# The sums of a windowed softmax: taken from ScalarE's accumulator instead of VectorE's reduction

## The chip, the cores and the metric

The kernel runs on one core of a Trainium2 chip. The metric is the time of one execution on the device, in microseconds (us); the span is the time from the first to the last instruction of the profiled execution. The engines are TensorE (PE; its weight loads are shown apart as PEld), VectorE (DVE), ScalarE (ACT), GpSimd (POOL) and SyncE (SP, which issues the transfers). Each engine works through its own queue in order and waits on semaphores for the others.

## The reference

Attention with a window and block summaries, and then two feed-forward layers on its result. Of the attention (2 batches, 8 heads, 768 positions, head size 64):

```python
scores_l = scale * np.matmul(q, k.transpose(0, 1, 3, 2))
mask_l = np.abs(pos[:, None] - pos[None, :]) < window            # window = 16
scores_s = scale * np.einsum('bhsd,bhnd->bhsn', q, k_sum) + np.log(block)
scores_all = np.concatenate([np.where(mask_l, scores_l, -1e9), scores_s], axis=-1)
scores_all = scores_all - np.max(scores_all, axis=-1, keepdims=True)
a = np.exp(scores_all)
a = a / (np.sum(a, axis=-1, keepdims=True) + 1e-09)
attn = np.matmul(a, np.concatenate([v, v_sum], axis=2))
```

Its 1536 x 512 result goes through `relu(x @ w_in) ** 2 @ w_out` (inner size 2048), and that through a second layer with a rational function in place of the squared relu.

## The kernel before

**The attention** is cut into 24 steps `d`, each for 2 x 128 queries of two heads. A step works on four slices `c` of 64 queries of two heads (128 rows) by 120 columns: 96 keys around the window and 24 block summaries. Its parts, with the letter that each has in the order below, are:

- `q`, `z`: PE transposes the queries, ACT copies them into `qz` (L445).
- `s`: PE makes the scores (four slices into one bank `pss`, L456).
- `m` (`d_m`, L471): per slice, DVE adds the mask, negates, and takes the minimum into column `c` of a small tile `mx` (128 x 8); the result goes to `pr`, a tile of 4 x 121 columns of which the last of each slice holds 1e-9.
- `e` (`d_e`, L480): per slice, ACT takes the exponential of `pr` in place, with column `c` of `mx` as bias. Below, e0 to e23 are these 24 groups of four exponentials.
- `r` (`d_r`, L488 and L489): DVE sums the 4 x 121 columns of `pr` into columns 4 to 7 of `mx` and takes the reciprocal into `rs`.
- `n` (L495): POOL multiplies the slices by `rs`; `p` (L505): PE transposes them; `b` (L509): ACT or DVE copies them to `pp`; `o` (L521): PE multiplies with the values; `x`, `y` (L535, L540): ACT casts the result to `xh`, DVE makes the remainder `xl`.

There are two buffers of `mx` and `rs` and three of `pr`.

**The feed-forward layers** multiply in three passes (high by high, high by low, low by high). `h` (L572) is the first multiplication of a layer, `i` (L585, ACT) its relu, `j` (L602, DVE) the square, `G` (L635, ACT) the cast to `sh`, `H` (L642, POOL) the remainder `sl`, `Y` (L666) the second multiplication. The weights arrive as 64-bit numbers and are made into a high and a low part by `T` (ACT, L150), `D` (DVE, L160 and L161), `W` (ACT, L172) and `M` (POOL, L177).

**The order** of attention, weights and the first layer's first pass is written out by hand in one string, `ORDER`, of a letter and a number for each part; each engine's queue follows it. After the string's end (at about 155 us) loops issue the rest. Near the start the string reads `... z5 s4 w0 p1 m4 o0 e4 r3 I1 I2 s5 z6 n2 Q2 p2 b1* B3* N2 T1 o1 m5 W0 ...`: W0 stands behind e0 to e4 in ACT's queue.

Of the kernel before, what the change touches and what calls it, by code (L numbers as in the profile page):

```python
# [12 lines left out]
ALU = mybir.AluOpType  # L13
I32 = mybir.dt.int32
AX = mybir.AxisListType
# [43 lines left out]
def tile_window_attention_moe_moe(  # L59
# [13 lines left out]
    nc = tc.nc  # L73
# [313 lines left out]
    def k_put(p, wins=slice(0, NWIN), copy=nc.vector.tensor_copy, first=True):  # L387

        p %= NP
        ks = kss[p]  # L390
        if first:
            nc.vector.tensor_reduce(
                out=ks.rearrange("p (w n) -> p w n", n=2),
                in_=kt[p][:, :, WIN:WIN + LO].rearrange("p w (n t) -> p w n t", t=BLK),
                axis=AX.X, op=ALU.max,
            )
        dst = kt[p][:, wins, WT:]
        copy(
            out=dst, in_=ks.rearrange("p (o n) -> p o n", o=1).to_broadcast([P, dst.shape[1], NB])
        )  # L400
# [76 lines left out]
    def d_e(d):  # L477
        mx, pr = ex[d] = pm.pop(d)
        for c in range(4):
            nc.scalar.activation(  # L480
                out=pr[:, c, 0:HK], in_=pr[:, c, 0:HK], func=AF.Exp, scale=-1.0,
                bias=mx[:, c:c + 1],
            )

    def d_r(d):
        mx, pr = ex.pop(d)
        rs = ap.tile([P, 4], F32, tag="rs", name="rs", bufs=2)
        nc.vector.tensor_reduce(out=mx[:, 4:8], in_=pr, axis=AX.X, op=ALU.add)  # L488
        nc.vector.reciprocal(out=rs, in_=mx[:, 4:8])  # L489
        pn[d] = rs, pr  # L490

# [229 lines left out]
    def w_next(j):  # L721
# [10 lines left out]
        c=lambda p: k_put(p, some, dve), B=lambda p, c=act: k_put(p, rest, c, False),  # L732
        S=lambda p: s_add(v0[p], LEFT) if p < NP else s_add(vst), V=v_sum,
        u=lambda h, c=act: v_put(h, 0, c), w=lambda h, c=act: v_put(h, 1, c),
        q=d_t, z=d_z, s=d_s, m=d_m, e=d_e, r=d_r, n=d_n, p=d_p, b=d_b, o=d_o, x=d_x, y=d_y,
        T=lambda k: w_next(0), D=lambda k: w_next(1), W=lambda k: w_next(2),
        M=lambda k: w_low(*divmod(k, 2)), O=lambda i: keep(("y0", "y1")),
# [47 lines left out]
    for g in range(G1, NG):  # L785
        ps, c, f = steps[g]
# [66 lines left out]
```

## Time and profile before

| | us |
|---|---|
| median of 3 runs | 620.4 (620.27 to 620.71) |
| profiled execution | 620.43 |
| its span | 618.5 |
| PE busy in the span | 600.2 (97%) |
| DVE busy / ACT busy / POOL busy | 407.6 / 403.2 / 356.4 |

The shares are averages over stages with different limits: the attention occupies the first 155 us, and the engines' shares there differ from those of the rest. PE's matmuls are pipelined, so a busy PE can still contain short waits.

### The profile page before, as it was taken

Reading aid. Unit: us, or ns where it says so; the run is one execution under the profiler, and the core shown is the slowest. Engines: PE = TensorE matmul, PEld = TensorE weight load, DVE = VectorE, ACT = ScalarE, POOL = GpSimd, SP = SyncE. Lnnn points to the kernel's source line nnn. Section 1 sums busy time; section 2 is a strip of 40 time slices with the busy share of each in tenths; the row PEclk is TensorE's granted clock in tenths of the full one; section 3 lists DMA queues with packets and bytes.
Section 4 is the critical chain, followed back from the end, with each engine's and each line's share of the span. In section 5 each row is a group of like instructions: output and inputs, shape, how many; then the busy total and the mean of one; then the engine's idle time right before and its main releaser. Section 6 shows DMA issues by size and latency. Waiting matters only on the chain.

```text
span 618.5 us, 9770 instructions
## 1 busy us (share of the span) xinstructions
PE 600.2 (97%) x3488; PEld 515.6 (83%) x3488; DVE 407.6 (66%) x810; ACT 403.2 (65%) x771; POOL 356.4 (58%) x363
## 2 busy tenths in 40 slices
PE   6789999999999999999999999999999999999997
PEld 5689999999988778888888888788888888888886
DVE  5988967855267762011247899978766977776673
ACT  5978667856265553112356998988778788777761
POOL 3878974545266665121477899855545754544451
PEclk9989999999999999999999999999999999999999
DMA  9979991730045550000016442310000000010011
GB/s 222 244 206 222 232 224 17 188 87 3 1 143 163 173 190 13 0 1 0 1 37 205 135 135 86 121 33 1 1 0 1 34 1 1 1 40 29 1 68 68
DMA packets 64143, 51.48 MB, mean 83 GB/s; under 512 B 39776, under 2 KB 56160, under 8 KB 64096
## 3 DMA queue, kind: packets, MB, share of 16 engines
q1 hardware_dynamic: 64096, 50.87, 30.5%
q8 instruction: 27, 0.44, 0.3%
q14 instruction: 20, 0.16, 0.1%
HBM read 47.71 MB, written 3.15 MB: 82 GB/s over the span
## 4 chain that ended last, share of the span: by engine, by line
PE 50%; DVE 7%; POOL 3%; ACT 2%; issue 1%; POOLq 0%; ACTq 0%; DVEq 0%
PE y L666 25%; PE h L572 25%; DVE wdec L161 2%; POOL wl L177 2%; POOL sl L642 1%; DVE acc L694 1%; DVE h L621 1%; ACT wdec L150 1%; DVE wdec L160 1%; DVE q L618 1%; DVE p L624 1%; DVE p L606 1%; DVE p L605 1%; ACT sh L635 0%; ACT wh L172 0%
## 5 line engine op out<-in xcount | busy, mean ns | idle before, releaser
L572 PE MATMUL h<-xh,wh 128*128 128x512 f32 (+1 forms) x444 | 162.3, 365 | 0.8 <-DVE r L602 0.4
L572 PE MATMUL h<-xl,wh 128*128 128x512 f32 (+1 forms) x444 | 160.1, 361 | 0.8 <-DVE xl L540 0.8
L572 PE MATMUL h<-xh,wl 128*128 128x512 f32 (+1 forms) x444 | 160.0, 360 | 0.0
L642 POOL TENSOR_TENSOR sl<-r,sh 128x512 fp32r<-128x512 f32 (+1 forms) x63 | 69.1, 1098 | 113.0 <-ACT sh L635 95.5
L593 POOL TENSOR_TENSOR q<-q,u 128x512 f32<-128x512 f32 x48 | 63.6, 1326 | 76.2 <-ACT q L590 76.2
L177 POOL TENSOR_TENSOR wl<-wdec,wh 128x512 fp32r<-128x512 f32 x64 | 87.5, 1375 | 25.6 <-ACT wh L172 25.6
L572 PEld LDWEIGHTS h<-xh,wh 128*128 128x128 f32 x444 | 83.7, 189 | 14.7 <-DVE p L624 1.1
L572 PEld LDWEIGHTS h<-xl,wh 128*128 128x128 f32 x444 | 83.8, 189 | 13.5 <-DVE xl L540 1.0
L602 DVE TENSOR_TENSOR r<-r,h 128x512 f32<-128x512 f32 (+1 forms) x63 | 35.0, 556 | 90.3 <-ACT r L585 90.3
L572 PEld LDWEIGHTS h<-xh,wl 128*128 128x128 f32 x444 | 83.7, 189 | 12.5
L666 PE MATMUL y<-sh,wh 128*128 128x512 f32 (+1 forms) x252 | 86.8, 345 | 1.6 <-ACT sh L635 1.6
L666 PE MATMUL y<-sh,wl 128*128 128x512 f32 (+1 forms) x252 | 85.2, 338 | 0.0
L666 PE MATMUL y<-sl,wh 128*128 128x512 f32 (+1 forms) x252 | 80.7, 341 | 0.3 <-POOL sl L642 0.3
L642 POOL TENSOR_TENSOR sl<-p,sh 128x512 fp32r<-128x512 f32 x48 | 64.9, 1353 | 20.5 <-ACT sh L635 16.9
L666 PE MATMUL y<-wl,sh 128*128 128x512 f32 x192 | 74.7, 389 | 0.0
L666 PE MATMUL y<-wh,sh 128*128 128x512 f32 x192 | 74.4, 389 | 0.0
L666 PE MATMUL y<-wh,sl 128*128 128x512 f32 x192 | 74.0, 389 | 0.0
L161 DVE SCALAR_TENSOR_TENSOR wdec<-wraw,wdec 128x512 int32<-128x512 int32 x64 | 68.7, 1073 | 1.7
L585 ACT ACTIVATE r<-h 128x512 f32<-128x512 f32 (+1 forms) x63 | 31.1, 494 | 47.4 <-PE h L572 26.1
L160 DVE TENSOR_SCALAR wdec<-wdec 128x512 int32<-128x512 int32 x64 | 46.4, 726 | 20.7 <-ACT wdec L150 20.6
L172 ACT CAST wh<-wdec 128x512 fp32r<-128x512 f32 x64 | 39.5, 621 | 28.8 <-DVE wdec L161 26.9
L635 ACT CAST sh<-r 128x512 fp32r<-128x512 f32 (+1 forms) x63 | 32.4, 514 | 38.9 <-PE y L666 38.6
(88 smaller groups left out, 1091.9 us busy)
## 6 DMA issues: line engine op xcount, KB each, us to landing
wraw<-in_moe_w_in_dram SPq DMA_DIRECT2D x32, 512.0 KB, 3.9
wraw<-in_moe_w_out_dram SPq DMA_DIRECT2D x32, 512.0 KB, 3.3
early<-in_v_dram SPq DMA_DIRECT2D x40, 96.0 KB, 4.3
out_dram<-acc SPq DMA_DIRECT2D x12, 256.0 KB, 2.1
acc<-in_q_dram SPq DMA_DIRECT2D x10, 256.0 KB, 7.1
early<-in_k_dram SPq DMA_DIRECT2D x4, 384.0 KB, 5.2
early<-in_v_dram SPq DMA_DIRECT2D x4, 384.0 KB, 7.2
kst<-in_k_dram SPq DMA_DIRECT2D x8, 192.0 KB, 6.3
```

The source lines that it names most:

```text
L150: x = nc.scalar.activation(out=f32(t), in_=f32(r[:, :, 1]), func=AF.Prelu, scale=2.0 ** -112, alpha=-(2.0 ** 32))
L160: nc.vector.tensor_single_scalar(out=t, in_=t, scalar=3, op=ALU.logical_shift_left)
L161: nc.vector.scalar_tensor_tensor(out=t, in0=low, scalar=29, in1=t, op0=ALU.logical_shift_right, op1=ALU.bitwise_or)
L172: nc.scalar.copy(out=wt[n][0][:, j], in_=f32(wdec[n, j]))
L177: nc.gpsimd.tensor_tensor(out=tl[:, j], in0=t, in1=f32(th[:, j]), op=ALU.subtract)
L572: nc.tensor.matmul(hq[g][:, 0:n], lhsT=w[:, 0, ws], rhs=x[:, part, ts], start=(part == 0 and j == 0), stop=(part == KC - 1 and j == 2),)
L585: nc.scalar.activation(out=r, in_=h, func=AF.Relu)
L593: nc.gpsimd.tensor_tensor(out=q_, in0=q_, in1=u_, op=ALU.mult)
L602: nc.vector.tensor_tensor(out=eq[g], in0=eq[g], in1=h, op=ALU.mult)
L635: nc.scalar.copy(out=sh[:, 0:n], in_=e)
L642: nc.gpsimd.tensor_tensor(out=sl[:, 0:n], in0=eq.pop(g), in1=f32(sh[:, 0:n]), op=ALU.subtract)
L666: x = nc.tensor.matmul(o, lhsT=lt, rhs=rt, start=(f == 0 and j == 0 and d * m % 512 == 0), stop=(f == FS[ps] - 1 and j == 2 and (d + 1) * ...
```

## The change

Each exponential also delivers the sum of its 120 results through ScalarE's accumulator, into column `4 + c` of `mx`. VectorE's reduction over 4 x 121 columns is replaced by an addition of 1e-9 to the four sums, in place; the reciprocal stays. The last column of `pr`, which held the 1e-9, is still filled and no longer read.

```diff
             nc.scalar.activation(
                 out=pr[:, c, 0:HK], in_=pr[:, c, 0:HK], func=AF.Exp, scale=-1.0,
                 bias=mx[:, c:c + 1],
+                accum_out=mx[:, 4 + c:5 + c],
             )
 
     def d_r(d):
         mx, pr = ex.pop(d)
         rs = ap.tile([P, 4], F32, tag="rs", name="rs", bufs=2)
-        nc.vector.tensor_reduce(out=mx[:, 4:8], in_=pr, axis=AX.X, op=ALU.add)
+        nc.vector.tensor_scalar_add(mx[:, 4:8], mx[:, 4:8], 1e-9)
         nc.vector.reciprocal(out=rs, in_=mx[:, 4:8])
```

No instruction of the program changes its place: the queues of PE, POOL and SP are the same row for row, ACT's has the exponentials in the same places with a second output, and DVE's has the addition where the reduction stood. The addition waits for ACT's four exponentials as the reduction did, and the reciprocal for the addition.

## Rows read from the trace of the kernel before

**Rows 1.** The page's line of busy time, share of the span and instructions.

```profile
PE 600.2 (97%) x3488; PEld 515.6 (83%) x3488; DVE 407.6 (66%) x810; ACT 403.2 (65%) x771; POOL 356.4 (58%) x363
```

**Rows 2.** Busy time by stretch, with granted clock and share of DMA.

```profile
core 0: us, PE busy (x) PEld busy (x) DVE busy (x) ACT busy (x) POOL busy (x), PEclk, DMA share, GB/s
13.00:28.00 15.00, 12.44 (x123) 10.97 (x122) 14.52 (x71) 13.72 (x38) 10.14 (x19) 1.00 1.11 266
28.00:37.00 9.00, 5.83 (x48) 5.14 (x47) 8.37 (x22) 6.04 (x19) 7.64 (x11) 0.99 0.95 240
37.00:66.00 29.00, 28.65 (x306) 27.36 (x307) 24.90 (x83) 24.02 (x63) 23.41 (x33) 0.94 0.95 204
66.00:155.00 89.00, 88.34 (x909) 85.85 (x909) 60.74 (x204) 60.49 (x164) 53.38 (x92) 1.00 0.51 120
```

**Rows 3.** Single lines: instructions, ns shortest/median/longest, first and last start, forms.

```profile
L480 ACT ACTIVATE pr<-pr,mx x96: 377/383/408, 13.1 to 147.2; 128x120 f32<-128x120 f32 x96
L488 DVE TENSOR_REDUCE mx<-pr x24: 642/652/658, 14.7 to 147.7; 128x4 f32<-128x484 f32 x24
L471 DVE DVE_READ_ACCUMULATOR2_ANT mx<- x96: 74/83/85, 13.0 to 146.8; 128x1 f32 x96
L796 ACT ACTIVATE abc<-ab x1: 191/191/191, 177.3 to 177.3; 128x2 f32<-128x2 f32 x1
L793 DVE TENSOR_SCALAR abc<-ab x2: 136/138/141, 178.3 to 178.4; 128x1 f32<-128x1 f32 x2
L398 DVE COPY kt<-kss x14: 211/248/1226, 8.8 to 111.5; 128x96 f32<-128x96 f32 x8, 128x192 f32<-128x192 f32 x6
```

**Rows 4.** ACT in order of time, 13 to 28 us: start, duration, instruction, [idle before].

```profile
13.07 1.25 ACT L480 ACTIVATE pr<-pr,mx 128x120 f32<-128x120 f32 x4 [0.78 <-DVE mx L471]
...
18.67 1.25 ACT L480 ACTIVATE pr<-pr,mx 128x120 f32<-128x120 f32 x4 [0.58 <-DVE mx L471]
...
24.13 0.63 ACT L419 COPY early<-pvs 24x256 f32<-24x256 f32 x2 [0.33 <-PE ptp L505]
24.79 1.25 ACT L480 ACTIVATE pr<-pr,mx 128x120 f32<-128x120 f32 x4
...
27.44 0.61 ACT L172 CAST wh<-wdec 128x512 fp32r<-128x512 f32 x1
```

**Rows 5.** POOL, DVE, ACT and PE in order of time, 28 to 38 us.

```profile
28.13 1.39 POOL L177 TENSOR_TENSOR wl<-wdec,wh 128x512 fp32r<-128x512 f32 x1 [0.73 <-ACT wh L172]
...
32.54 1.27 POOL L177 TENSOR_TENSOR wl<-wdec,wh 128x512 fp32r<-128x512 f32 x1
32.84 1.26 DVE L160 TENSOR_SCALAR wdec<-wdec 128x512 int32<-128x512 int32 x1
...
34.90 0.78 DVE L419 COPY early<-pvs 24x256 f32<-24x256 f32 x2
35.76 0.63 ACT L419 COPY early<-pvs 24x256 f32<-24x256 f32 x2 [2.90 <-DVE early L419]
36.41 0.59 ACT L509 COPY pp<-ptp 120x512 f32<-120x512 f32 x1
37.05 1.97 PE L521 MATMUL pav<-pp,early 120*64 120x64 f32 x32 [2.22 <-ACT pp L509]
```

**Rows 6.** Later places of the same pattern: ACT, POOL and PE in order of time.

```profile
55.25 1.25 POOL L642 TENSOR_TENSOR sl<-r,sh 128x256 fp32r<-128x256 f32 x1 [1.00 <-ACT sh L635]
...
99.46 1.25 ACT L480 ACTIVATE pr<-pr,mx 128x120 f32<-128x120 f32 x4 [0.81 <-DVE mx L471]
100.74 0.39 ACT L585 ACTIVATE r<-h 128x256 f32<-128x256 f32 x1
101.02 0.40 ACT L635 CAST sh<-r 128x256 fp32r<-128x256 f32 x1
101.57 0.73 POOL L642 TENSOR_TENSOR sl<-r,sh 128x256 fp32r<-128x256 f32 x1 [2.24 <-ACT sh L635]
102.35 0.19 PEld L666 LDWEIGHTS y<-sl,wh 128*128 128x128 f32 x1 [0.16 <-POOL sl L642]
...
145.46 0.73 POOL L642 TENSOR_TENSOR sl<-r,sh 128x256 fp32r<-128x256 f32 x1 [3.24 <-issue]
```

**Rows 7.** From the waits of ACT and PE, 0 to 155 us: total, times, longest.

```profile
ACT r L585 <- PE h L572: 9.2, 9, 1.8
...
PE ptp L505 <- POOL pr L495: 0.3, 1, 0.3
```

## The prediction

> **What bounds the kernel.** I start at the line of busy time: PE works in 97% of the span, so an edit on DVE and ACT counts only where PE waits for them [rows 1]. The edit touches nothing behind 155 us, so I read the stretches of the attention [rows 2]. From 13 to 28 us PE leaves 15.00 − 12.44 = 2.6 us idle, from 28 to 37 us 3.2 us; there DVE (14.52 of 15) and ACT (13.72 of 15) have almost nothing free. From 37 to 155 us PE is busy but for 0.35 + 0.66 us, and ACT is busy 24.0 of 29 us and then 60.5 of 89. So the start is paced by the small engines; later PE paces, and what counts there is whether a result that PE needs arrives in time.
>
> PE's longest wait after its first instruction is 2.22 us, at 37.05 us, for `pp` [rows 5]. I followed it backwards: ACT's copy L509 (36.41) stood behind ACT's copy L419, which waited 2.90 us for DVE's L419 (34.90); that stood behind DVE's L160 and L161, of which L160 (32.84) ran until 34.10, behind POOL's L177 (32.54 to 33.81). POOL had worked without a gap since 28.13, when its first L177 had waited 0.73 us for ACT's cast L172. So the wait at 37.05 hangs on one ACT instruction, L172, which started at 27.44 [rows 4]. Ahead of it in ACT's queue stand e0 to e4, the first at 13.07 and the last at 24.79, and from 13.07 to 27.44 the trace shows ACT idle for only 0.58 + 0.33 us. Whatever a group e costs more, L172 pays five times, less 0.91 us.
>
> **What DVE gains.** 24 reductions of 652 ns go [rows 3]. The addition over four columns does not occur in the trace; its nearest row is a TENSOR_SCALAR over 128x1 (a multiplication) of 138 ns. That would free 24 × (0.652 − 0.138) = 12.3 us of DVE. The upper bound comes from another row: DVE's copy L398 took from 211 to 1226 ns, while all 24 reductions lie between 642 and 658. The page SBUF — State Buffer of the Trainium skill ("Who interferes with whom") has a rule that speaks against this change: a `tensor_scalar` or copy inside SBUF can need the port pair that DVE shares with GpSimd and then waits for GpSimd's whole instruction, a `tensor_reduce` never. The spread of the copies and the lack of one in the reductions agree with it. At 1.23 us each the additions would cost DVE 24 × 0.57 = 13.9 us more instead of freeing 12.3. I take 0.14 to 0.7 us, so about half of the gain. None of it reaches PE on the chain above: between POOL's start at 28.13 and DVE's L419, DVE waits for POOL, and before 28.13 ACT decides.
>
> **What ACT pays.** Each of 96 exponentials has to hand out its accumulator. The trace has no such row for ACT; DVE's L471 shows what a delivery looks like there, a second instruction of 83 ns behind each. I call the extra ACT time per exponential t.
> - Nothing is the lower bound: DVE's read lies wholly in the tail of the instruction before it.
> - Four exponentials take 1.25 us, one takes 0.383, so they follow each other at (1.25 − 0.383)/3 = 0.289 us, overlapping by 0.094 [rows 3, 4]. ACT's shortest instruction is the 128x2 ACTIVATE of 0.191 us. If the read is such an instruction and overlaps like the others, t = 0.191 − 0.094 = 0.097.
> - If it takes that row's full time, t = 0.191; if the exponential must in addition drain before it, t = 0.191 + 0.094 = 0.285, the upper bound.
>
> I take 0.19: the read is a small instruction on the same engine, so the ACT row is nearer than the DVE row, and an instruction that needs the finished sum can hardly overlap the exponential that forms it. A group then costs 4 × 0.19 = 0.76 us more, ACT in all 18 us.
>
> On the overlap the Trainium skill has a rule (ScalarE: Activation LUTs, "What ACT_TABLE_LOAD costs"): an ACTIVATE with a pointer as bias takes about 280 ns and 0.833 ns per element, one without pointers 186 ns, and neighbours overlap by about 93 ns. The 383 ns and the 0.094 us of the rows agree. An estimate by that page for a pointerless read of one element is 187 − 93 = 94 ns; by it the sum would be that of the second rival.
>
> **The sum.** (1) The wait at 37.05: 5 × 0.76 − 0.91 = +2.9 us. e5 and e6, behind L172, add 1.5 us that fit into ACT's 2.90 us of idle time ahead of 35.76 [rows 5]. (2) Later groups. At e14 (99.46) ACT's L585 and L635 follow at once, POOL's remainder L642 waits for L635, and PE's weight load at 102.35 already waits 0.16 us for L642 [rows 6]: 0.76 us more in ACT are 0.76 us more in PE. By the order in which ACT's instructions stand behind the groups I count six such places: e8 with e9 (remainder at 55.25), e12 with e13, e14, e17, e18 with e19, e21 (remainder at 145.46). At the others ACT waits next for something else anyway: nine times, 9.2 us in all, its relu L585 waits for PE [rows 7], about 1.0 us each, which hides a group. A place with two groups owes up to 1.5 us, less the small slack there; an estimate from the pattern is 0.7 us each, 6 × 0.7 = 4.2 us. (3) DVE's gain: 0. Together +7.1 us.
>
> The profiled execution took 620.43 us, which is the median of the runs (620.4) to within its spread; 620.4 + 7.1 = **627.5 us**.
>
> **The rivals.**
> - *The read is hidden* (t below 0.075). The point is where term 1 vanishes, t = 0.91/20 = 0.046; at 0.075 it is 0.6 us, and six places owe 0.3 us each less slack, some 0.6 us: the 1.24 us that make 0.2%, about what a measurement of this kernel can tell from no change. With t = 0, reduction and addition alone differ: the reduction of e0 ends 0.4 us earlier, POOL and DVE's copies behind it as well, and part of it reaches 37.05: 620.0 us. For it speaks DVE's read; against it that ACT's small instruction is more than twice as long [rows 3].
> - *Half price* (t about 0.10): 20 × 0.097 − 0.91 = 1.0 us, and six places at 0.39 less slack, about 0.2 each: 1.2 us. 622.6 us.
> - *Full drain* (t = 0.285): 20 × 0.285 − 0.91 = 4.8, and six places at about 1.05: 6.3. 631.5 us.
> - *The addition waits for POOL*, on top of the forecast: PE waits for POOL's `pr` at one place only (0.3 us) [rows 7], so a delay of 0.57 us of the reciprocal would show at two or three places: +1.5, 629.0 us. The port rule above is its ground; against it, POOL itself often waits for the reciprocal and is then free.
>
> **Chances.** Forecast 0.42, half price 0.24, hidden 0.20, full drain 0.10, addition 0.04. Slower by over 0.2%: the forecast, the drain, the addition and most of half price, which stands only 1 us above the bound (0.19 of 0.24): 0.75. Within 0.2%: the rest of half price and most of the hidden case: 0.20. Faster: 0.05, where the hidden read meets a gain of DVE over 1.24 us. The range reaches from a read almost hidden (620.5) to the full drain (631.5). The likeliest case alone has 625 to 629.5.
>
> **What would show it.** Right: the four exponentials of a group last about 2.0 us instead of 1.25, with 96 new small ACT rows; L172 starts near 30.3 instead of 27.44, POOL's L177 near 31.0, and PE's wait for `pp` ends near 40; the weight load behind e14's remainder waits about 0.9 us instead of 0.16. Behind 155 us every stretch is as long as before. On DVE 24 rows near 0.14 us, some stretched to POOL's end. Wrong: a group e still near 1.3 us, or L172 late and 37.05 not, which would mean that POOL, DVE or a transfer held that chain for another reason; or new PE waits behind DVE's addition.

## The result, and the profile after

| | before | after |
|---|---|---|
| median, us | 620.34 (619.88 to 620.71, 4 runs) | 623.40 (623.02 to 624.59, 4 runs) |
| profiled execution, us | 620.43 | 623.02 |
| its span, us | 618.5 | 621.1 |
| ratio, 95% interval | | 1.0056 (1.0043 to 1.0069) |

The change makes the kernel slower by 3.1 us. The forecast had the direction and the two places; it had more than twice the size (+7.1 us).

The line of busy time after the change, beside [rows 1]:

```profile
PE 601.0 (97%) x3488; PEld 515.8 (83%) x3488; DVE 398.4 (64%) x810; ACT 411.3 (66%) x867; POOL 356.5 (57%) x363
```

ACT has 96 instructions more and 8.1 us more of busy time, DVE 9.2 us less. PE's busy time grows by 0.8 us, so 1.8 of the 2.6 us of span are waits of PE. By stretch, beside [rows 2]:

```profile
13.00:28.00 15.00, 11.74 (x116) 10.08 (x113) 11.95 (x68) 14.68 (x58) 10.24 (x19) 1.00 1.12 261
28.00:37.00 9.00, 6.65 (x54) 5.79 (x50) 7.76 (x20) 6.24 (x25) 7.51 (x11) 1.00 0.88 209
37.00:66.00 29.00, 27.12 (x293) 25.96 (x294) 23.00 (x83) 25.10 (x78) 21.87 (x32) 0.94 0.97 209
66.00:155.00 89.00, 87.46 (x875) 84.73 (x875) 55.19 (x202) 64.90 (x219) 55.18 (x93) 1.00 0.51 122
```

From 13 to 28 us ACT goes from 13.72 to 14.68 of 15 us, DVE from 14.52 to 11.95. DVE's relief is real, and it is in the stretch where DVE had nothing free; now ACT has almost nothing free there. From 37 to 155 us PE is idle for (29.00 − 27.12) + (89.00 − 87.46) = 3.4 us, against 1.0 us before; 1.1 us of it is the end of the wait for `pp`, which now reaches beyond 37 us.

The single lines that answer to [rows 3] (line numbers behind 482 are higher by one):

```profile
L480 ACT ACTIVATE pr<-pr,mx x96: 378/382/407, 12.9 to 150.9; 128x120 f32<-128x120 f32 x96
L480 ACT ACTIVATION_READ_ACCUMULATOR pr<-pr,mx x96: 185/187/200, 13.2 to 151.2; 128x1 f32 x96
L489 DVE TENSOR_SCALAR mx<-mx x24: 159/170/1209, 14.5 to 151.4; 128x4 f32<-128x4 f32 x24
```

The exponential itself is as long as before. Behind each stands a read of the accumulator of 187 ns, about what the prediction took from the 0.191 us row. How the reads lie in time decides the size; ACT's first group:

```profile
12.85 0.40 ACT L480 ACTIVATE pr<-pr,mx 128x120 f32<-128x120 f32 x1 [0.79 <-DVE mx L471]
13.15 0.18 ACT L480 ACTIVATION_READ_ACCUMULATOR pr<-pr,mx 128x1 f32 x1
13.24 0.38 ACT L480 ACTIVATE pr<-pr,mx 128x120 f32<-128x120 f32 x1
13.53 0.19 ACT L480 ACTIVATION_READ_ACCUMULATOR pr<-pr,mx 128x1 f32 x1
13.62 0.38 ACT L480 ACTIVATE pr<-pr,mx 128x120 f32<-128x120 f32 x1
```

The exponential of 13.24 ends at 13.62, its read starts at 13.53, and the next exponential at 13.62, when the read still has 0.10 us to run. The read overlaps the exponential ahead of it and the one behind it by some 0.09 us each. From start to start it is 0.38 us, where it was 0.289 [rows 3, 4]: t = 0.38 − 0.289 = **0.091 us**, not 0.19.

The chain to PE's wait for `pp`, which [rows 4, 5] show for the kernel before:

```profile
27.95 0.61 ACT L172 CAST wh<-wdec 128x512 fp32r<-128x512 f32 x1
28.64 1.73 POOL L177 TENSOR_TENSOR wl<-wdec,wh 128x512 fp32r<-128x512 f32 x1 [1.26 <-ACT wh L172]
32.61 2.55 DVE L160 TENSOR_SCALAR wdec<-wdec 128x512 int32<-128x512 int32 x1 [0.42 <-ACT wdec L150]
32.93 1.26 POOL L177 TENSOR_TENSOR wl<-wdec,wh 128x512 fp32r<-128x512 f32 x1
34.18 1.97 POOL L496 TENSOR_SCALAR pr<-pr,rs 128x120 f32<-128x120 f32 x4
35.95 0.78 DVE L419 COPY early<-pvs 24x256 f32<-24x256 f32 x2
36.82 0.63 ACT L419 COPY early<-pvs 24x256 f32<-24x256 f32 x2 [2.72 <-DVE early L419]
37.46 0.58 ACT L510 COPY pp<-ptp 120x512 f32<-120x512 f32 x1
38.10 1.09 PE L522 MATMUL pav<-pp,early 120*64 120x64 f32 x30 [3.21 <-ACT pp L510]
```

It is the same chain, later: L172 by 0.51 us, POOL's L177 by 0.51, DVE's L419 by 1.05, PE by 1.05. In this execution e0 began 0.22 us earlier than before (12.85 against 13.07), so the five groups pushed L172 back by 0.73 us relative to their own start. Between L177 and L419 something was added that the prediction did not have: DVE's L160 came at 32.61 instead of 32.84, had just begun when POOL's L177 (32.93) and then its L496 (34.18) took over, and ended only at 35.16 (before: 34.10). DVE arrived earlier, and spent what it had gained, and more, beside POOL. From L172's start to the end of PE's wait it is 10.15 us here and 10.20 in the second profile of the change (change_again), against 9.61 before. In e1_act_pays (below) the reduction stays, L160 lasts 1.29 us, and the same way takes 9.52 us:

```profile
28.45 0.62 ACT L172 CAST wh<-wdec 128x512 fp32r<-128x512 f32 x1
...
33.73 1.29 DVE L160 TENSOR_SCALAR wdec<-wdec 128x512 int32<-128x512 int32 x1
...
37.97 1.98 PE L522 MATMUL pav<-pp,early 120*64 120x64 f32 x32 [2.25 <-ACT pp L510]
```

So at this place the relief of DVE costs about 0.5 us.

### The profile page after: what moved, and what is told of

Read it like the earlier page. It is cut to its first block, busy times and chain, and to the rows that moved or that the text cites. A ratio compares the mean times of both kernels' runs of the same rounds, so it can differ in the third digit from the quotient of the medians.

```text
span 621.1 us, 9873 instructions
## 1 busy us (share of the span) xinstructions
PE 601.0 (97%) x3488; PEld 515.8 (83%) x3488; DVE 398.4 (64%) x810; ACT 411.3 (66%) x867; POOL 356.5 (57%) x363
## 4 chain that ended last, share of the span: by engine, by line
PE 50%; DVE 7%; ACT 2%; POOL 2%; issue 1%; DMA 1%; POOLq 0%; ACTq 0%; SPq 0%; DVEq 0%
PE y L667 25%; PE h L573 25%; DVE wdec L161 2%; POOL wl L177 1%; POOL sl L643 1%; ACT wdec L150 1%; DVE acc L695 1%; DVE h L622 1%; DVE wdec L160 1%; DVE q L619 1%; DVE p L607 1%; DVE p L625 1%; DVE p L606 1%; DMA wraw<-in_moe_w_out_dram 1%; ACT sh L636 1%
## 5 line engine op out<-in xcount | busy, mean ns | idle before, releaser
L177 POOL TENSOR_TENSOR wl<-wdec,wh 128x512 fp32r<-128x512 f32 x64 | 87.3, 1372 | 27.3 <-ACT wh L172 27.3
L160 DVE TENSOR_SCALAR wdec<-wdec 128x512 int32<-128x512 int32 x64 | 47.0, 735 | 21.3 <-ACT wdec L150 21.3
L586 ACT ACTIVATE r<-h 128x512 f32<-128x512 f32 (+1 forms) x63 | 31.0, 493 | 44.4 <-PE h L573 24.3
L172 ACT CAST wh<-wdec 128x512 fp32r<-128x512 f32 x64 | 39.5, 621 | 28.3 <-DVE wdec L161 26.3
```

Of the source, the lines that this page charges most:

```text
L160: nc.vector.tensor_single_scalar(out=t, in_=t, scalar=3, op=ALU.logical_shift_left)
L172: nc.scalar.copy(out=wt[n][0][:, j], in_=f32(wdec[n, j]))
L177: nc.gpsimd.tensor_tensor(out=tl[:, j], in0=t, in1=f32(th[:, j]), op=ALU.subtract)
L586: nc.scalar.activation(out=r, in_=h, func=AF.Relu)
```

## The experiments

Theory A: the loss is ACT's extra time per exponential, 0.091 us, at the places that the prediction named, and DVE's relief is worth nothing. Its rival, theory B: the addition, a new link between ACT's sums and POOL's multiplication, holds up the chain. Two more came with the runs and are put in their expectations: C, that the early delay is swallowed later, and D, that the addition costs because it waits for POOL. The ratios are against the kernel before, run on the same chip beside each series; its medians there are 620.44 us (e1 to e4), 620.06 (e5 to e8) and 620.37 (the last four rows). A ratio is not the quotient of two medians: the medians of e5_first_five differ by 2.1 us, its ratio stands for 1.3 us.

| kernel | median, us | ratio, 95% interval |
|---|---|---|
| e1_act_pays | 624.35 | 1.0060 (1.0048 to 1.0072) |
| e2_dve_gains | 620.09 | 0.9994 (0.9984 to 1.0003) |
| e3_twice | 628.54 | 1.0124 (1.0109 to 1.0139) |
| e4_no_add | 621.89 | 1.0021 (1.0010 to 1.0031) |
| e5_first_five | 622.16 | 1.0021 (1.0007 to 1.0036) |
| e6_from_six | 621.88 | 1.0029 (1.0015 to 1.0043) |
| e7_warm_after | 622.98 | 1.0038 (1.0026 to 1.0050) |
| e8_warm_before | 620.51 | 1.0001 (0.9988 to 1.0013) |
| change_again | 623.81 | 1.0053 (1.0034 to 1.0071) |
| e10_add_as_reduce | 622.70 | 1.0038 (1.0025 to 1.0052) |
| e11_add_behind | 623.60 | 1.0054 (1.0040 to 1.0069) |
| e9_one_exp | 622.11 | 1.0024 (1.0012 to 1.0035) |

**e1_act_pays: ACT's part alone.** The exponentials deliver their sums, and the reduction stays (shown against the change).

```diff
-        nc.vector.tensor_scalar_add(mx[:, 4:8], mx[:, 4:8], 1e-9)
+        nc.vector.tensor_reduce(out=mx[:, 4:8], in_=pr, axis=AX.X, op=ALU.add)
```

> ScalarE delivers the sums, but VectorE still makes its reduction and overwrites them: ScalarE's part of the change alone. Theory A (ScalarE's extra 0.091 us per exponential is the price, VectorE's gain is worth nothing on the path): as slow as the change or a little slower, 623.0 to 624.5 us. Theory B (the price is VectorE's: the addition, or VectorE running earlier into GpSimd's instructions): near the kernel before, 620.3 to 621.5 us.

Measured: 3.9 us slower, as theory A has it. ACT's reads alone make the whole loss; the interval overlaps the change's.

**e2_dve_gains: DVE's part alone.** The kernel before, with the addition (on the last exponential of each slice) in place of the reduction, so that the softmax is not normalised.

```diff
-        nc.vector.tensor_reduce(out=mx[:, 4:8], in_=pr, axis=AX.X, op=ALU.add)
+        nc.vector.tensor_scalar_add(mx[:, 4:8], pr[:, :, HK - 1], 1e-9)
```

> VectorE's part of the change alone: no accumulator on ScalarE; the addition reads the last exponential of each slice instead of the sums, so the softmax is not normalised rightly, only the work is the same. Theory A: as the kernel before or slightly faster, 619.6 to 620.6 us. Theory B: 621.5 to 623 us.

Measured: no difference, as theory A has it. DVE's busy time falls by 6.3 us (407.6 to 401.3; by 9.2 in the change), and no time comes back: the third term of the sum, DVE's gain at 0, holds as long as ACT has no reads to make. The additions are in this kernel too, one of them stretched to 1194 ns, and cost nothing that can be seen.

**e3_twice: the price doubled.** The change, with a further 128x1 instruction of ACT behind each read.

```diff
                 accum_out=mx[:, 4 + c:5 + c],
             )
+            nc.scalar.copy(out=jk[:, 4 * d + c:4 * d + c + 1], in_=mx[:, c:c + 1])
```

> The change with one more ScalarE instruction of 128x1 behind each exponential, a copy into a tile of its own: about 0.19 us per exponential in all, the price that the prediction took. If the prediction's sum was right and only the price wrong: about 627.5 us (625 to 629.5). If the sum over-counted the later places: 624.5 to 625.5 us.

Measured: 8.1 us slower. ACT's rows of it, and the chain:

```profile
13.59 0.40 ACT L481 ACTIVATE pr<-pr,mx 128x120 f32<-128x120 f32 x1 [0.78 <-DVE mx L472]
13.89 0.19 ACT L481 ACTIVATION_READ_ACCUMULATOR pr<-pr,mx 128x1 f32 x1
13.99 0.17 ACT L486 COPY jk<-mx 128x1 f32<-128x1 f32 x1
14.07 0.39 ACT L481 ACTIVATE pr<-pr,mx 128x120 f32<-128x120 f32 x1
...
30.53 0.60 ACT L172 CAST wh<-wdec 128x512 fp32r<-128x512 f32 x1
...
40.04 1.50 PE L524 MATMUL pav<-pp,early 120*64 120x64 f32 x32 [2.56 <-ACT pp L512]
```

The exponentials now follow each other at some 0.47 us (13.59, 14.07, and so on), so t = 0.18, nearly the 0.19 that the prediction had used. L172 stands 30.53 − 13.59 = 16.94 us behind e0, 2.57 more than the 14.37 before; the first term gives 20 × 0.18 − 0.91 = 2.7. PE's wait ends at 40.04, 2.99 us later than before; counted from e0 it is 2.47 us later (26.45 against 23.98). The whole is 8.1 us, inside the first expectation; the sum had 7.1 at t = 0.19. So this kernel pays nearly the price that the prediction assumed, and the sum comes out about 1 us short of the measured time, as the half price does for the change (2.2 against 3.1).

**e5_first_five and e6_from_six: the two terms apart.** The change for `d < 5` alone and for `d >= 5` alone; the other groups keep the reduction. In e5_first_five:

```diff
-                accum_out=mx[:, 4 + c:5 + c],
+                accum_out=mx[:, 4 + c:5 + c] if d < 5 else None,
...
-        nc.vector.tensor_scalar_add(mx[:, 4:8], mx[:, 4:8], 1e-9)
+        if d < 5:
+            nc.vector.tensor_scalar_add(mx[:, 4:8], mx[:, 4:8], 1e-9)
+        else:
+            nc.vector.tensor_reduce(out=mx[:, 4:8], in_=pr, axis=AX.X, op=ALU.add)
```

> The change for the first five groups alone (accumulator and addition for d < 5, reduction for the rest). Theory A, that the loss of 3.1 us is made of separate places, each of which keeps the delay of the exponentials ahead of it: the place at 37 us alone, which cost about 1.05 us in the change's profile, perhaps with 0.5 us from the later fall of the clock: 621.3 to 622.0 us. Theory C, that the first delay is swallowed later, because PE has idle time left between 37 and 66 us that a later start of PE's work uses up: 620.2 to 620.8 us.

> The other part of it: the accumulator and the addition for d >= 5, the reduction for the first five. Theory A: the six later places alone, 1.5 to 2 us, 622.0 to 622.5 us; its gain or loss and that of the first five together make about the change's 3.1 us. Theory C, that the early part is swallowed: about 623.2 us, the whole loss.

Measured: 0.21% and 0.29%, together 0.50% of the change's 0.53 to 0.56%. The medians lie 0.16 us above theory A's range (e5_first_five) and 0.12 us below it (e6_from_six). Both parts lose, and they add up. Theory C falls with e6_from_six, whose interval ends 0.5 us below its 623.2 us, and with the profile of e5_first_five: counted from e0, POOL's remainders start 1.1 us later than before at 45 us, and 1.3 us later at 150 us, so the early delay is not swallowed. The first five by their rows of ACT:

```profile
12.47 0.40 ACT L480 ACTIVATE pr<-pr,mx 128x120 f32<-128x120 f32 x1 [0.29 <-DVE mx L471]
...
27.59 0.61 ACT L172 CAST wh<-wdec 128x512 fp32r<-128x512 f32 x1
```

and the kernel with the others:

```profile
12.94 1.25 ACT L480 ACTIVATE pr<-pr,mx 128x120 f32<-128x120 f32 x4 [0.78 <-DVE mx L471]
...
27.30 0.60 ACT L172 CAST wh<-wdec 128x512 fp32r<-128x512 f32 x1
```

L172 stands 15.12 us behind e0 in the first and 14.36 in the second; 15.10 in the change, 15.16 in e1_act_pays (13.29 to 28.45), 14.37 before. The delay of L172 is a matter of the five groups' accumulator reads alone, to within 0.1 us, whether DVE reduces or adds.

**e4_no_add, e10_add_as_reduce and e11_add_behind: what the addition costs.** The change without the addition; with a reduction over one element each in its place; and with the addition behind the reciprocal.

```diff
-        nc.vector.tensor_scalar_add(mx[:, 4:8], mx[:, 4:8], 1e-9)
```

```diff
-        nc.vector.tensor_scalar_add(mx[:, 4:8], mx[:, 4:8], 1e-9)
+        nc.vector.tensor_reduce(out=mx[:, 4:8], in_=mx[:, 4:8].rearrange("p (c o) -> p c o", o=1), axis=AX.X, op=ALU.add)
```

```diff
-        nc.vector.tensor_scalar_add(mx[:, 4:8], mx[:, 4:8], 1e-9)
         nc.vector.reciprocal(out=rs, in_=mx[:, 4:8])
+        nc.vector.tensor_scalar_add(mx[:, 4:8], mx[:, 4:8], 1e-9)
```

> The change without the addition of 1e-9 (24 VectorE instructions fewer; the sums are at least 1, so the result stays the same in float32). Theory A: as the change within 0.4 us. Theory B in the form that the addition waits for GpSimd and holds up the chain: 1 to 2 us faster than the change.

> The change itself once more, so that the next three are compared with it on one chip. All theories: 623.0 to 623.8 us.

> The change with the addition of 1e-9 as a reduction over one element each (128x4 out of 128x4x1; the 1e-9 is not added, which leaves a sum of 1 or more as it is in this format). The same number of instructions on the same chain of results, but of a kind that was never stretched beside POOL in these traces. Theory D, that the addition costs because it waits for POOL's instructions: about 622 us, near the kernel without the addition, and 24 rows of nearly one length. Theory B, that it costs because it is one more link of the chain: 623.0 to 623.6 us, as the change.

> The change with the addition behind the reciprocal, on sums that nobody reads any more: DVE does the same instructions, but the reciprocal does not wait for the addition. Theory B (one more link ahead of POOL's multiplication): 621.5 to 622.3 us, as without the addition. Theory D (DVE's time and its waits for POOL, wherever the addition stands): 623 us or more.

Measured: without the addition 1.0021, as a reduction 1.0038, behind the reciprocal 1.0054, the change beside the last two 1.0053. e4_no_add is 1.5 us below the change, so theory A's expectation missed and theory B's was met; e10_add_as_reduce lies between its two expectations; e11_add_behind lies where theory D has it, and theory B's there missed. change_again, at 623.81 us, is at the upper end of its range. First the reduction of e10_add_as_reduce, by its line:

```profile
L489 DVE TENSOR_REDUCE mx<-mx x24: 148/157/159, 13.8 to 150.3; 128x4 f32<-128x4 f32 x24
```

then the addition of e11_add_behind, by its line, and one place of it in order of time:

```profile
L490 DVE TENSOR_SCALAR mx<-mx x24: 170/171/2734, 14.6 to 153.8; 128x4 f32<-128x4 f32 x24
```

```profile
25.08 1.27 POOL L329 TENSOR_TENSOR early<-early 96x512 f32<-96x512 f32 x1 [1.45 <-DMA early<-in_v_dram]
25.21 1.17 DVE L490 TENSOR_SCALAR mx<-mx 128x4 f32<-128x4 f32 x1
```

The addition that began 0.13 us behind a POOL instruction ended with it; behind the reciprocal, where POOL has just been released, one lasted 2.73 us. Of the reductions none was stretched. So the addition does wait for POOL, and moving it off the chain of results brings nothing. What that costs in time is not settled: e10_add_as_reduce and the change differ by 1.1 us in the median, inside their intervals. Without the addition the time is 1.5 us below the change's median, outside its interval, but the profile does not place that gain. Its span is 1.0 us shorter (620.1 against 621.1), and 0.90 us of that are there when e0 starts (11.95 against 12.85), before any instruction that was edited. The first scores of that execution, and of the change's:

```profile
10.09 1.08 PE L456 MATMUL pss<-kt,qz 128*128 128x120 f32 x8
```

```profile
10.53 1.96 PE L456 MATMUL pss<-kt,qz 128*128 128x120 f32 x8
```

The same eight matmuls took little more than half the time. From e0 on the two profiles are alike: L172 stands 15.11 us behind e0 (15.10 in the change), and the span ends 608.15 us behind e0 (608.25; before, 605.43). So a part of the 1.5 us may be a matter of how the executions began; one profile cannot say it of all ten runs.

e1_act_pays and e4_no_add differ in DVE's reduction alone, and their intervals do not overlap (1.0060 and 1.0021). So with the reads in ACT's queue DVE's work is no longer free, though e2_dve_gains shows it free without them. How much of the 2.5 us between the two lies behind e0 is open: their profiles differ by 0.7 us there (608.81 and 608.15).

**e7_warm_after and e8_warm_before: is it the clock?** The granted clock falls for a few microseconds about 40 us, and the change moves that place. In 2 us stretches, before, and then after:

```profile
36.00:38.00 2.00, 0.95 (x18) 0.95 (x20) 0.54 (x2) 1.99 (x6) 0.41 (x1) 0.71 0.76 264
38.00:40.00 2.00, 2.00 (x25) 1.88 (x22) 1.82 (x3) 1.39 (x6) 2.00 (x3) 0.50 0.04 8
```

```profile
38.00:40.00 2.00, 1.30 (x33) 1.17 (x33) 0.82 (x1) 1.95 (x6) 1.35 (x2) 0.95 0.40 147
40.00:42.00 2.00, 2.00 (x10) 2.00 (x11) 1.93 (x7) 1.46 (x4) 2.00 (x5) 0.50 0.00 0
```

0.50 is the lower of TensorE's two levels, 1.2 GHz. Both kernels were given repeats `F` of step 4's four transposes ahead of the wait, seven in the change and four in the kernel before:

```diff
+    def d_f(d):
+        pr = prs[d % NPR]
+        for c in range(4):
+            nc.tensor.transpose(
+                out=po[d][0:HK, c * P:(c + 1) * P], in_=pr[:, c, 0:HK], identity=ident
+            )
...
-  ... q8 p4 w1 M1 ...
+  ... q8 p4 F4 F4 F4 F4 F4 F4 F4 w1 M1 ...
```

> The change, with seven repeats of step 4's four transposes (28 matmuls, results overwritten with the same values) ahead of PE's long wait, so that PE does not stand idle there. In the change's profile the granted clock is at its lower level in 39.8 to 43.2 us, on work that PE itself paces; in the kernel before it is low in 36.9 to 40.3 us, of which PE would have waited a good part anyway. If that shift of the low clock is part of the loss (about 0.9 to 1.3 us), this runs in 622.0 to 622.6 us and its profile has no low stretch there. If the clock has no part in it, 623.2 to 623.8 us.

> The kernel before with four such repeats at the same place, the counterpart: its low stretch lies mostly on time in which PE waits, so it should gain less than the changed kernel does. If the clock's shift is part of the loss: 619.5 to 620.4 us. If the repeats are only more work or do nothing: 620.3 to 621.0 us.

Measured: 622.98 us, between the two expectations, and 620.51 us, in the range of the repeats doing nothing. With the repeats the changed kernel's clock stays up; two of its stretches:

```profile
38.00:40.00 2.00, 1.65 (x37) 1.27 (x35) 0.24 (x1) 1.97 (x6) 0.77 (x1) 1.00 0.55 215
40.00:42.00 2.00, 1.28 (x9) 1.08 (x9) 1.94 (x4) 1.43 (x4) 2.00 (x4) 1.00 0.00 0
```

Eight of its twelve executions had a mean granted clock of 1.0, and they took 622.1 to 624.6 us, 623.0 in the mean. The kernel before gains nothing from the repeats. Between the two kernels with repeats 2.5 us remain, so most of the loss stands with the clock up. A share of the clock of up to 1 us is not excluded by the intervals.

**e9_one_exp: ACT's time shortened instead.** The kernel before, with one exponential for all four slices and the least of their four minima as bias.

```diff
+        nc.vector.tensor_reduce(out=mx[:, 4:5], in_=mx[:, 0:4], axis=AX.X, op=ALU.min)
...
-        for c in range(4):
-            nc.scalar.activation(
-                out=pr[:, c, 0:HK], in_=pr[:, c, 0:HK], func=AF.Exp, scale=-1.0,
-                bias=mx[:, c:c + 1],
-            )
+        nc.scalar.activation(
+            out=pr[:, :, 0:HK], in_=pr[:, :, 0:HK], func=AF.Exp, scale=-1.0, bias=mx[:, 4:5]
+        )
```

> The kernel before with ScalarE's time per group shortened in place of lengthened: one exponential over 4 x 120 columns with the least of the four minima as bias (one small extra reduction of 4 columns on DVE), the sums by the reduction as before. By the rows of before one such exponential takes about 0.38 + 360 x 0.000833 = 0.68 us, against 1.25 for the four. Theory A, that ACT's time ahead of L172 sets the wait for pp at 37 us in this direction too: a part of 5 x 0.5 us is gained there until DVE takes over as the bound, and some at the later places: 617.5 to 619.5 us. Rival, that DVE, which has almost nothing free from 13 to 28 us, is the bound at once: 620.0 to 621.0 us.

Measured: 622.11 us, 0.24% slower, so both expectations missed. Its costliest group on ACT, and the start of its first step:

```profile
L480 ACT ACTIVATE pr<-pr,mx 128x480 f32<-128x480 f32 x24 | 16.6, 696 | 14.7 <-DVE mx L475 14.7
```

```profile
12.70 0.28 DVE L471 CUSTOM_DVE_ANT_0 pr<-pss,mask 128x120 f32<-128x120 f32 x1 [0.70 <-PE pss L456]
...
13.63 0.16 DVE L475 TENSOR_REDUCE mx<-mx 128x1 f32<-128x4 f32 x1
...
13.82 0.69 ACT L480 ACTIVATE pr<-pr,mx 128x480 f32<-128x480 f32 x1 [1.06 <-DVE mx L475]
```

The exponential takes 0.70 us, as expected, and ACT saves 24 × (1.25 − 0.70) = 13 us. But it cannot start before the fourth slice and the extra reduction are done: it ends 13.82 + 0.69 − 12.70 = 1.8 us after DVE's first slice began; before, the four ended 13.07 + 1.25 − 12.74 = 1.6 us after it. The saving became waiting (14.7 us behind L475; before, 4.5 us behind L471). Four short exponentials that follow DVE slice by slice are the better form here; what share of the loss is the extra reduction on DVE is not separated. None of these kernels is faster than the kernel before beyond the noise.

## Why the prediction was wrong in size

**The bound and the chain held.** PE paces, and the edit shows at PE's wait for `pp` and at later places: e1_act_pays has the loss, e2_dve_gains has no gain, and e5_first_five and e6_from_six divide the loss into those two parts.

**The step that failed is the price t.** The prediction took 0.19 us because "an instruction that needs the finished sum can hardly overlap the exponential that forms it". The rows show that it does: it starts 0.09 us before the exponential's end, and the next exponential starts 0.10 us before its end. Measured, t is 0.091 us. This is the rival *half price* (0.097 us, 622.6 us), and its sentence "if the read is such an instruction and overlaps like the others" describes what happened. The Trainium skill (ScalarE: Activation LUTs, "What ACT_TABLE_LOAD costs") gives 186 ns and 0.833 ns per element for an ACTIVATE without pointer and an overlap of about 93 ns between neighbours, from which the prediction had an estimate of 94 ns; the read's 187 ns and the 0.091 us agree with it, though the page speaks of ACTIVATEs and not of the read. The guess about a dependence had no row; the overlap of ACT's neighbours had one (0.094 us in [rows 4]), and it was the better guide.

**Term 1**, 20t − 0.91, gives 0.91 us at the measured t. L172 came 0.73 us later behind e0, and the first five groups alone cost 0.21% (0.07 to 0.36%), 1.3 us. In e3_twice, with t = 0.18, formula and row are 2.7 and 2.57 us. The term was right, and was fed with the wrong t. PE's wait ended 1.05 us later, 1.27 counted from e0: the 0.5 us beyond L172's delay are those of L160.

**Term 2**, six places at 4.2 us, fell with t to the 1.2 us of the half price; the groups from the sixth on cost 0.29% (0.15 to 0.43%), 1.8 us. At the place that the prediction named, e14, the remainder and PE's weight load are now:

```profile
101.28 0.40 ACT L480 ACTIVATE pr<-pr,mx 128x120 f32<-128x120 f32 x1 [0.87 <-DVE mx L471]
...
102.93 0.38 ACT L586 ACTIVATE r<-h 128x256 f32<-128x256 f32 x1
...
103.76 0.73 POOL L643 TENSOR_TENSOR sl<-r,sh 128x256 fp32r<-128x256 f32 x1 [2.77 <-ACT sh L636]
...
104.54 0.19 PEld L667 LDWEIGHTS y<-sl,wh 128*128 128x128 f32 x1 [0.58 <-POOL sl L643]
```

From the group's start to L586 it is 1.65 us, where it was 1.28 [rows 6]: 0.37 us more, four times 0.091. The weight load waits 0.58 us instead of 0.16: 0.42 us more. Here the mechanism is as described, at half the size that was expected (0.9 us), and at twice the 0.2 us that the half price allowed a place.

Not all six places did this. The remainders behind e12 with e13, before and then after, and the one behind e21 after (145.46 before, [rows 6]):

```profile
95.76 0.73 POOL L642 TENSOR_TENSOR sl<-r,sh 128x256 fp32r<-128x256 f32 x1 [3.06 <-ACT sh L635]
```

```profile
97.51 0.75 POOL L643 TENSOR_TENSOR sl<-r,sh 128x256 fp32r<-128x256 f32 x1 [3.06 <-ACT sh L636]
...
148.50 0.73 POOL L643 TENSOR_TENSOR sl<-r,sh 128x256 fp32r<-128x256 f32 x1 [3.61 <-issue]
```

Counted from each profile's e0 (13.07 and 12.85), the remainder behind e12 with e13 starts 2.0 us later than before, as the remainders from 63 us on do: this place adds nothing. Those behind e14, e17, e18 with e19, and e21 start 2.4, 2.6, 2.9 and 3.3 us later, so these four add 1.3 us. From 1.3 us at the wait for `pp` to 2.0 us at 63 us it is 0.7 us, of which the sixth place, e8 with e9, is only a part.

**Term 3**, DVE's gain at 0, held as a measurement without the reads (e2_dve_gains). The reason given for it, that DVE waits for POOL ahead of L419, is what the chain of after shows, and there the relief even costs 0.5 us: L160 came earlier and lasted 2.55 instead of 1.26 us. The prediction had no term for that. With the reads the 0 is not shown to hold over the whole kernel: without the reduction and the addition (e4_no_add) the loss is 1.5 us, with the reduction (e1_act_pays) 3.9.

**The sum.** The half price gave +2.2 us; +3.1 were measured in the first comparison and +3.4 in the second (620.37 to 623.81). In the two profiles the place of `pp` has 1.27 us and the later places 2.0, where the half price has 1.0 and 1.2; 0.4 us are won back before the end. That is one execution of each kernel, and others of the change differ: in change_again, whose granted clock from 37 to 66 us was 0.88 (0.94 in the first profile), the first remainder is already 3.2 us late, where it was 1.6. So how much of the rest belongs to the addition's waits, to L160 and to the clock is not settled.

**The rivals.** *The read is hidden* falls with e1_act_pays. *Full drain* falls with the rows: nothing drains. *The addition waits for POOL* is seen (159 to 1209 ns, 274 ns in the mean, within the 0.14 to 0.7 us that the prediction took), but its price of 1.5 us is not shown: e4_no_add is faster by just that, and its profile does not place it behind e0. A new wait did come: DVE now waits longer for ACT's sums. The waits of DVE after, and then before:

```profile
DVE mx L489 <- ACT pr L480: 10.6, 12, 1.7
```

```profile
DVE mx L488 <- ACT pr L480: 3.3, 7, 0.7
```

The 7.3 us more of waiting are most of the 9.2 us by which DVE's busy time fell. Most of DVE's gain became idle time in front of the engine that was lengthened.

## What to carry to other kernels

A sum "for free" from an accumulator is an instruction on the engine that delivers it: cost it in start-to-start time of that engine, with the overlap that its neighbours show, before asking what the relieved engine gains. Then see which of the two engines the next wait hangs on: here 0.48 us off DVE per step bought nothing by itself, and 0.36 us on ACT per step came through where PE was already waiting, or nearly so, for what ACT's queue delivers. Work that followed its producer slice by slice was not improved by fusing it (e9_one_exp), even though that saved the engine's time.

## What the runs showed that was not expected

- ScalarE's accumulator read (187 ns) overlaps the exponential whose sum it reads, and adds only 0.091 us from start to start. The exponential with the accumulator is as long as without (382 and 383 ns).
- A DVE instruction can be held up beside more than one POOL instruction: L160's 2.55 us (0.40 us where nothing stretches it) span all of L177 (32.93 to 34.19) and part of the four L496, and the addition in e11_add_behind lasted 2.73 us, longer than any L177 there (1.27 to 1.75 us).
- Executions of one kernel that showed a lower mean granted clock tended to be longer. Of the 34 executions of the kernel before that ran beside e5 to e8, the 7 with 0.993 or 0.994 took 621.0 to 622.5 us (mean 621.9), the 27 others 619.1 to 621.2 (mean 620.0). Beside e1 to e4 it was 4 executions (mean 621.3) against 17 (620.4); beside the last four kernels a single one, at 620.65, within the range of the others. The 6 of the 34 at 0.996, the clock of the profiled execution, took 619.8 us in the mean, so a low stretch as short as its own costs nothing that can be seen.
- The first scores of an execution took 1.08 us in one run and 1.96 us in another, at a clock that the view gives as 1.00 in both; e0 began 0.9 us earlier in the first. At 39.85 us in the profile of after, where the granted clock was 0.50 from 40 to 42 us, eight such matmuls took 2.06 us, and 1.15 us at 147.72 us, at 1.00. So the longer start looks like the lower clock level, but no record of the clock shows it.
